# A gated mix of two attentions: the gate moved between partitions by VectorE, long transfers planned by their queue, and q, k and phi awaited by halves

## The chip, the cores and the metric

The kernel runs on one core of a Trainium2 chip. A core has TensorE (PE; its weight loads are listed as PEld), VectorE (DVE), ScalarE (ACT), GpSimd (POOL) and SyncE (SP), which here issues all DMAs, in order, on one queue. The metric is the device time of the core in microseconds, median of the runs. The profile shows one more execution, with every instruction's start and duration, and names instructions by engine and line of the kernel (L709 is line 709).

## What is computed

The reference takes x of 2048 rows by 640 and mixes the outputs of two attentions with 32 heads of 20 elements each, row by row:

```
g = sigmoid((x * gate_w).sum(-1))            # one number per row
a = A_ref(x): 4 segments of 512 rows. Per segment and head
      causal softmax attention within the segment, and
      num = phi(q) M,  den = phi(q) z + 1e-6   # memory of earlier segments
      o   = sigmoid(beta) * num/den + (1 - sigmoid(beta)) * softmax part
      M  += phi(k)^T v,  z += sum phi(k)        # phi(t) = t+1 if t>0 else exp(t)
    then @ A_wo
b = B_ref(x): causal attention in a window of 256 rows, then @ B_wo
out = g * a + (1 - g) * b
```

All inputs are float32. The softmax subtracts each row's maximum.

## The kernel before, in words

The work is cut into 16 tiles T: 4 segments s of 512 rows, and within each four groups g of 16 heads, in the order A, B, A, B (g = 0, 2, 1, 3; `head`). A tile is four units u of 4 heads, 64 units in all. For each tile PE makes the projections of q and k (`plan_qk`: five blocks m of 128 rows; L432) and of v (`plan_v`: four blocks b of 128 rows; L553), with the operands split into a high and a low part, which ACT and POOL prepare (L381, L397) from transfers that line 389 issues: x and the weights wv come by `xst`, the weights wqk and wo by `wst`, a ring of two. q and k are then split into three bfloat16 parts and stored to DRAM (`qk_store`, L487, tensors dq and dk), and read back transposed into stacks of 120 partitions (`stack_read`, L616 and L619; three reads for q and three for k per unit). In the 640 rows of q and k of a tile, rows 0 to 319 belong to its units 0 and 1, rows 320 to 639 to units 2 and 3. phi of q and k takes the same way (`phl_store`, `phi_store`; read by `mem_stack`, L756, and `mem_load`, L748).

For each unit PE computes the scores once for the maxima (`max_mm`, L644, three PSUM banks), DVE reduces them (L655), and POOL, ACT and DVE split and transpose the maxima, which go to DRAM and back as three more rows of the query stack (`max_store`, L682, tensor dmx; `max_rows`, L686). Then PE computes the scores again with the maximum subtracted (`st_mm`, L709), ACT takes the exponential (L716), POOL masks (L722), PE multiplies with v (`av_mm`, L739), DVE turns the result (L820), which is scaled, turned back and stored (o_dram, L860). The output projections load it again (L873).

The gate: `wv` of group 0 has a further column, gate_w, so that column 320 of its v projection is the gate's logit. `z_out` (L562) copies it into `zg`, rows on 128 partitions. After the fourth block, once per segment, `z_store` (L566) writes it to DRAM and `z_load` (L570) reads it back as `zc`, where partition 32h + e holds rows 32i + e, i = 0 to 15, the same for each h, as the turned outputs lie. `z_exp` (ACT, L574) and `z_sig` (DVE, L578 to L580) make g and 1 - g; `fac` and `den_mul` multiply them into the scale of the outputs.

**What sets the order.** Nothing of this is in the order of the text. Each step is handed to a planner with `add(t, engine, duration, function, ...)`, where t is when it is due in units (unit u starts at u), and `new`, `put`, `mod` and `get` name the buffers it takes, fills, changes and reads. `Plan.order` is a list scheduler: it keeps a clock for each engine and for 16 DMA rings, and issues next the step that can start first; among those that can start at the same time, the one due first. The result is one program order per engine; on the chip semaphores hold each step until its data are there. For a DMA the planner adds its cost on each ring, `size / packet / rings * (0.011 + packet / 21e3)`, to what the ring still has. The constants that matter here: AHEAD 4.26 (how many units ahead of its tile a projection is due), PACE 2.18 (how far projections may run ahead of the scores), RD 2.5 (how far ahead the stacks are read), MT 1.3 and MS 0.58 (how far ahead the maxima and their splitting are due).

Of the kernel before, what the change touches and what calls it, by code (L numbers as in the profile page):

```python
# [22 lines left out]
L = 512  # L23
# [12 lines left out]
NK, NQ, NP, NX = 4, 4, 3, 5  # L36
NMX, NPJ, NST, NW, NO = 3, 3, 2, 2, 5
NPX, NMI, NOB = 7, 2, 2
AHEAD, RD, PACE = 4.26, 2.5, 2.18
TL, OZ, WL = 1.16, 5, 0.006  # L40
P0, MA, DP, NF, NR = 3.97, 0.94, 0.0, 1, 2
MT, MS = 1.3, 0.58
WARM = 26
LM, LR, LA, AT = 0.99, 2.03, 0.0, 0.11
DM, XP, XO, XS = 0.9, 0.32, 0.2, 0.11
OA = {5: 2, 6: 3, 7: 2, 8: 2, 9: 2, 10: 2, 11: 3, 12: 3, 13: 2, 14: 2, 15: 2}
AV = ((0, 1, 2),)
EPS = 1e-6


# [4 lines left out]
class Plan:  # L55
# [38 lines left out]
    def order(self):  # L94
# [7 lines left out]
        for i, (t, _, eng, dur, fn, a, new, mod, put, get, size, pace, cols, _, bank, _, _) in enumerate(items):  # L102
            if pace == "beat":
                beats.append((t, i))
            elif pace is not None:
                j = bisect.bisect_left(beats, (t - pace, 0)) - 1
                if j >= 0:
                    deps[i].add(beats[j][1])
            def slot(name):
                k = home.get(name, name)  # L110
                s = state.setdefault(k, {"who": name, "base": None, "puts": [], "gets": []})
                assert s["who"] == name, (fn, a, name, s["who"])
                return s
            for tag, bufs, name in new:
                c = count.get(tag, 0)
                count[tag] = c + 1
                k = (tag, "slot", c % bufs)
                home[name] = k
                s = state.get(k)
                if s:  # L120
                    deps[i] |= set(s["puts"]) | set(s["gets"])
                    if s["base"] is not None:
                        deps[i].add(s["base"])
                if tag in last_new:
                    assert after[last_new[tag]] is None
                    after[last_new[tag]] = i
                    order[i] = order.get(i, 0) + 1
                last_new[tag] = i
                state[k] = {"who": name, "base": i, "puts": [], "gets": [], "free": set(deps[i])}
            if bank:  # L130
                kind[bank[2]] = bank[0]
                state[bank[2]] = {"who": bank[2], "base": i, "puts": [], "gets": [], "free": set()}
                left[bank[2]] = 1
                uses[i].append(bank[2])
            for name in (*mod, *put, *get):
                if name in left:
                    left[name] += 1
                    uses[i].append(name)
            for name in mod:
                s = slot(name)  # L140
                deps[i] |= set(s["puts"]) | set(s["gets"])
                if s["base"] is not None:
                    deps[i].add(s["base"])
                s["base"], s["puts"], s["gets"] = i, [], []
            for name in put:
                s = slot(name)
                deps[i] |= set(s["gets"])
                if s["base"] is not None:
                    deps[i] |= s["free"] if name[0] in ("q", "k", "qf", "mst", "pk") else {s["base"]}
                s["puts"].append(i)  # L150
            for name in get:
                s = slot(name)
                deps[i] |= set(s["puts"])
                if s["base"] is not None:
                    deps[i].add(s["base"])
                s["gets"].append(i)
            deps[i].discard(i)
# [22 lines left out]
        while len(out) < n:  # L180
            best = None
            for e, c in cand.items():
                cold = e == "pe" and self.cold(free[e])
                for i in c:
# [10 lines left out]
                        z = max(z, min(avail.values()))  # L195
                    if e == "dve" and "|" in items[i][2]:
                        z += DP
                    z = (z, cold and items[i][12] < 900, i)
                    if best is None or z < best[0]:
                        best = (z, e)  # L200
# [58 lines left out]


@with_exitstack
def gated_mix_kernel(ctx: ExitStack, tc: tile.TileContext, xt, wqk, wv, wo, beta, ident, out):
    nc = tc.nc
    ctx.enter_context(tc.manual_schedule())
    const = ctx.enter_context(tc.tile_pool(name="const", bufs=1))
    dram = ctx.enter_context(tc.tile_pool(name="dram", bufs=1, space=DRAM))

    o_dram = [dram.tile([H, 32, S], F32, name=f"o_dram{i}") for i in range(2)]
    attention(ctx, tc, const, dram, xt, wqk, wv, wo, beta, ident, o_dram, out)


def attention(ctx, tc, const, dram, xt, wqk, wv, wo, beta, ident, o_dram, out):
    nc = tc.nc
    wpool = ctx.enter_context(tc.tile_pool(name="weights", bufs=1))
    xpool = ctx.enter_context(tc.tile_pool(name="xs", bufs=1))
# [13 lines left out]
        for i in range(WARM):  # L289
            nc.tensor.matmul(p[:, 0:256], ones[:, 0:128], ones, start=True, stop=True)  # L290

    idf = const.tile([128, 128], F32, name="idf")

    mask_a = const.tile([128, 512], BF16, name="mask_a")
    mask_b = const.tile([128, 384], BF16, name="mask_b")

# [12 lines left out]
    gh = const.tile([128, 2, 8], F32, name="gh")  # L309

    def c_load():
        nc.sync.dma_start(idf, ident)
        nc.sync.dma_start(bet, bass.AP(tensor=beta.tensor, offset=beta.offset, ap=[[8, 4], [0, 32], [1, 8]]))

    def c_exp():
# [37 lines left out]
        nc.gpsimd.memset(kst[i][96:128, p], -1.0)  # L353

    zg = const.tile([128, 16], F32, name="zg")
    dz = [dram.tile([L], F32, name=f"dz{i}") for i in range(NSEG)]
    zc = const.tile([128, 2, 2, 16], F32, name="zc")

    plan = Plan()
# [164 lines left out]
    def plan_qk(t, dt, T, m):  # L524
# [1 line left out]
        g, s = head(T)  # L526
        plan_gemm(t, dt, k, ("x", s), wqk[g, m])
        t += NC * dt - 0.01
        ph, dk = ("phi", T, m), ("dq", T)
        plan_parts(t + 1e-4, k, k)  # L530
        add(t + 3e-4, SP, SI * len(runs_of(m)), qk_store, T, m, put=[dk], get=[("hl", k)], size=3 * 2 ** 17, packet=1024)
        nk = rows_of(m, 1) if g < 2 and s < NSEG - 1 else 0
        nq = rows_of(m, 0) if g < 2 and s else 0
        if nk or nq:
# [2 lines left out]
            add(t + 6e-5, DVE, 0.61, phi_sum, T, m, get=[k], mod=[ph])  # L537
        if nk:
            add(t + 7e-4, SP, SI * len(runs_of(m, (1,))), phi_store, T, m, get=[ph],
                new=[("dphi", 2, ("dphi", T))] if m == 1 else [], put=[("dphi", T)] if m > 1 else [], size=2048 * nk)  # L540
        if nq:
            plan_parts(t + 8e-4, ph, ph)
            add(t + 1e-3, SP, SI * len(runs_of(m, (0,))), phl_store, T, m, get=[("hl", ph)],
                new=[("dphq", 2, ("dphq", T))] if m == 0 else [], put=[("dphq", T)] if m else [], size=3072 * nq, packet=1024)

    def v_mm(T, b, c):
        if c == 0:
# [14 lines left out]
        nc.vector.tensor_copy(zg[:, 4 * s + b:4 * s + b + 1], B["v", T, b][:, 16 * DH:16 * DH + 1])  # L562


    def z_store(s):
        nc.sync.dma_start(bass.AP(tensor=dz[s].tensor, offset=dz[s].offset, ap=[[1, 4], [16, 32], [4, 4]]),  # L566
                          zg[:, 4 * s:4 * s + 4])

    def z_load(s):
        nc.sync.dma_start(zc[:, s % 2, 0], bass.AP(tensor=dz[s].tensor, offset=dz[s].offset,  # L570
                                                   ap=[[0, 4], [16, 32], [1, 16]]))

    def z_exp(s):
        nc.scalar.activation(zc[:, s % 2, 0], zc[:, s % 2, 0], AF.Exp, scale=-1.0)  # L574

    def z_sig(s):
        z = zc[:, s % 2, 0]
        nc.vector.tensor_scalar(z, z, 1.0, None, op0=ALU.add)  # L578
        nc.vector.reciprocal(z, z)
        nc.vector.tensor_scalar(zc[:, s % 2, 1], z, -1.0, 1.0, op0=ALU.mult, op1=ALU.add)  # L580

    def va(T, b):

# [3 lines left out]
    def plan_v(t, dt, T, b):  # L587
# [8 lines left out]
        if g == 0:  # L596
            add(t + 1e-4, DVE, 0.08, z_out, T, b, get=[k], put=["zg"])
            if b == 3:
                add(t + 2e-4, SP, DI, z_store, s, get=["zg"], put=[("dz", s)], size=2048, packet=4)
                add(t + 3e-4, SP, DJ, z_load, s, get=[("dz", s)], new=[("z", 2, ("z", s))], size=8192, packet=64, rings=4)  # L600
                add(t + 4e-4, ACT, 0.25, z_exp, s, mod=[("z", s)])
                add(t + 5e-4, DVE, 0.7, z_sig, s, mod=[("z", s)])

# [336 lines left out]
            add(-14 + i, POOL, 0.7, init_k, i, p, put=[("ik", i)])  # L942
    add(-13, POOL, 2.0, c_mask, put=["mk"])
    add(-25, PE, 0.107 * WARM, c_warm, bank=("warm", 1, "warm"), cols=256 * WARM)
    add(-16.5, SP, 1.1, c_load, put=["cl"], size=2 ** 16)
    add(-3, ACT, 0.25, c_exp, get=["cl"], put=["ce"])
    add(-3, DVE, 1.2, c_fac, get=["cl", "ce"], put=["cf"])

# [3 lines left out]
    for T in range(NT + 2):  # L952
# [38 lines left out]
        for u in range(4 * T, 4 * T + 4):  # L991
            tr = u - RD
            for i in range(3):
                for w in range(2):
# [1 line left out]
                    ring = [] if i else [("qk"[w] + "st", (NQ, NK)[w], k)]  # L996
                    b, c = RUNS[w][i]
                    add(tr, SP, DI, stack_read, u, w, b, c, new=ring, put=[] if ring else [k],
                        get=[("dq", T)] + ([("dq", T - NSG)] if w and back(T) else []) +
                        ([("ik", u % NK)] if ring and w else []),  # L1000
                        size=c * 8 * n, packet=2 * n if w and head(T)[0] >= 2 else 4096, rings=RINGS[c])
                    tr += 1e-3
# [8 lines left out]
    for u in range(NU):  # L1011
# [55 lines left out]
        if not isb:  # L1067
            if s > 0:
                for i in range(3):
                    qk = ("qf", u)  # L1070
                    add(u + 0.3 + 0.001 * i, SP, DI, mem_stack, u, i, get=[("dphq", T)],
                        new=[] if i else [("qf", NF, qk)], put=[qk] if i else [], size=RUNS[0][i][1] * 4096, packet=4096, rings=RINGS[RUNS[0][i][1]])
                add(te + 0.02, PE, 0.25, mem_read, u, get=[("qf", u), ("mst", T - NSG)], bank=("misc", NMI, ("num", u)),
                    cols=2048, ldw=(0.027, 0.02), lazy=LR)
                add(te + 0.03, DVE, 0.64, o_turn, u, 1, get=[("num", u)], put=[ok])
            if s < NSEG - 1:
                for i in range(4):
                    add(u - 0.3 + 0.001 * i, SP, DI, mem_load, u, i, get=[("dphi", T), "im"],
                        new=[] if i else [("pk", 1, ("pk", u))], put=[("pk", u)] if i else [], size=DH * 2048, packet=128, rings=10)
                add(u + 0.3, DVE, 0.63, mem_turn, u, get=[("pk", u)], new=[("pkn", 1, ("pkn", u))])  # L1080
                add(u + MA, PE, 0.57, mem_add, u, ldw=(0.027, 0.02), lazy=LM, get=[("pkn", u)] + [("va", T, b) for b in range(4)], bank=("madd", 1, ("madd", u)))
# [21 lines left out]
def layout(A_x, A_wq, A_wk, A_wv, A_wo, A_beta, B_x, B_wqkv, B_wo, gate_w):  # L1103
# [16 lines left out]
    def turn(w):  # L1120
        return w.reshape(NC, 128, NC, 128).transpose(2, 1, 0, 3).reshape(NC, 128, D)
    return dict(xt=n(n(A_x)[0].T), wqk=n(np.stack([turn(w) for w in qk])), wv=n(np.stack(vv)),
                wo=n(np.stack([turn(w) for w in (n(A_wo)[rows], n(B_wo)[rows], n(B_wo))])),
                beta=n(n(A_beta).reshape(8, 4).T), ident=np.eye(128, dtype=np.float32))


# [13 lines left out]
```

## Time and profile before

| what | value |
|---|---|
| median of 3 runs | 1178.53 us (1175.38 to 1179.56) |
| the profiled execution | 1183.04 us |
| its span, first to last instruction | 1181.3 us |
| granted PE clock, mean | 0.979 |
| PE, DVE, ACT, POOL busy | 93%, 66%, 60%, 69% |
| DMA moved | 224.24 MB, 190 GB/s on average |

In the views of the profile a row of a group gives line, engine, operation, tiles written <- read, shape and count, then the busy time, the mean duration of one in ns, the idle time of the engine just ahead of them and who ended it. A row of the waits gives: who waited <- for whom: us in total, times, the longest. A row of the windows gives start:end, length, then busy time (and count) of PE, PEld, DVE, ACT and POOL, the granted PE clock as a share of full speed, the busy share of the 16 DMA engines, and GB/s. A row of the instructions of a tile gives shortest/median/longest in ns, first and last start.

### The profile page before, as it was taken

What the parts mean: (1) busy time and instruction counts of PE and PEld (TensorE: products, weight loads), DVE (VectorE), ACT (ScalarE), POOL (GpSimd) and SP (SyncE); (2) the same over time, 40 slices, a digit from 0 to 9 for tenths busy, and PEclk for the clock granted to TensorE, in tenths of its full rate; (3) what the DMA queues carried; (4) which work ended last, traced back from release to release, by engine and by line L of the source; (5) the groups of instructions that cost most, each with busy time, mean ns of one, the idle gap of its engine ahead of it and who ended that gap; (6) DMA issues with size and microseconds to landing.
All of it is one profiled execution on the core that took longest, in us unless ns stands there. A gap on an engine that the chain in (4) does not pass through costs nothing.

```text
span 1181.3 us, 25003 instructions
## 1 busy us (share of the span) xinstructions
PE 1093.2 (93%) x8322; PEld 718.9 (61%) x8322; DVE 778.6 (66%) x2640; ACT 704.6 (60%) x1496; POOL 816.1 (69%) x1063
## 2 busy tenths in 40 slices
PE   9789999997999999989798999997979899999996
PEld 7565666664556666656465666665646557665564
DVE  3477887665768667976666866676647577567711
ACT  6246756675467755567454776646636477645661
POOL 9436674786568776688655877667757587756874
PEclk9989999998999999999899999999999999999999
DMA  6868878778887599777787868887588676788423
GB/s 212 171 180 195 220 195 206 186 192 183 218 204 197 143 210 253 200 193 219 160 219 188 204 167 220 209 209 178 156 171 223 172 206 160 220 202 216 137 91 107
DMA packets 194753, 224.24 MB, mean 190 GB/s; under 512 B 80768, under 2 KB 143616, under 8 KB 194624
## 3 DMA queue, kind: packets, MB, share of 16 engines
q1 hardware_dynamic: 194624, 222.64, 73.9%
q8 instruction: 66, 1.08, 0.4%
q14 instruction: 63, 0.52, 0.2%
HBM read 157.62 MB, written 64.95 MB: 188 GB/s over the span
## 4 chain that ended last, share of the span: by engine, by line
PE 52%; DMA 29%; DVE 6%; POOL 5%; ACT 3%; SPq 3%; issue 2%; POOLq 0%; DVEq 0%; ACTq 0%
PE bank L432 19%; PE bank L709 9%; PE bank L553 8%; PE bank L739 8%; PE bank L644 8%; DMA qst<-dmx 5%; DMA dmx<-mt 5%; DMA qst<-dq 4%; DMA xst<-wv 3%; DMA kst<-dk 3%; DVE bank L655 3%; DMA wst<-wqk 2%; DMA xst<-o_dram 2%; ACT P L716 1%; DMA pks<-dphi 1%
## 5 line engine op out<-in xcount | busy, mean ns | idle before, releaser
L716 ACT ACTIVATE P<-bank 128x512 f32<-128x512 f32 (+2 forms) x768 | 374.1, 559 | 121.6 <-PE bank L709 101.2
L432 PE MATMUL bank<-xhl,w 128*128 128x512 f32 x1200 | 363.8, 429 | 1.4 <-DVE xhl L397 0.4
L655 DVE CUSTOM_DVE_ANT_0 bank<-bank,mask_b 128x384 f32<-128x384 f32 (+2 forms) x512 | 260.2, 549 | 65.0 <-PE bank L644 63.9
L644 PE MATMUL bank<-kst,qst 120*128 120x384 bf16 (+3 forms) x1024 | 258.9, 314 | 33.8 <-DVE mx L655 12.8
L655 DVE CUSTOM_DVE_ANT_0 bank<-bank,mask_a 128x128 f32<-128x128 f32 (+3 forms) x512 | 238.2, 511 | 74.9 <-PE bank L644 73.6
L709 PE MATMUL bank<-qst,kst 123*128 123x384 bf16 (+2 forms) x1216 | 231.8, 293 | 38.6 <-DMA qst<-dmx 29.8
L397 POOL TENSOR_TENSOR w<-wst,w 128x640 fp32r<-128x640 f32 x119 | 185.4, 1558 | 92.5 <-ACT w L381 92.2
L432 PEld LDWEIGHTS bank<-xhl,w 128*128 128x128 f32 x1200 | 218.9, 192 | 46.1 <-issue 1.9
L722 POOL TENSOR_SCALAR_AFFINE_SELECT P<-P 128x512 f32<-128x512 f32 x256 | 161.0, 636 | 86.1 <-ACT P L716 80.2
L553 PE MATMUL bank<-wv,xhl 128*128 128x320 f32 (+1 forms) x960 | 194.9, 337 | 0.7 <-POOL wv L397 0.2
L432 PE MATMUL bank<-ohl,w 128*128 128x512 f32 x600 | 178.8, 425 | 6.5 <-POOL w L397 2.7
L709 PEld LDWEIGHTS <-kst 123*128 123x128 bf16 x1216 | 91.9, 99 | 142.3 <-issue 70.8
L644 PEld LDWEIGHTS <-qst 120*128 120x128 bf16 x1024 | 82.9, 99 | 131.1 <-issue 94.6
L739 PE MATMUL bank<-P,vau 128*32 128x384 f32 (+3 forms) x2432 | 159.9, 407 | 1.2 <-DVE mt L789 0.8
L553 PEld LDWEIGHTS bank<-wv,xhl 128*128 128x128 f32 x960 | 153.7, 192 | 11.4 <-DVE mx L655 1.4
L655 DVE DVE_READ_ACCUMULATOR2_ANT mx<- 128x1 f32 x1024 | 143.2, 140 | 0.0
L451 POOL TENSOR_TENSOR hl<-res,hl 128x512 bf16<-128x512 f32 x104 | 121.1, 1166 | 23.7 <-ACT hl L381 19.9
L820 DVE STREAM_TRANSPOSE ot<-bank 128x512 f32<-128x512 f32 x88 | 62.7, 713 | 108.5 <-PE bank L739 98.1
L432 PEld LDWEIGHTS bank<-ohl,w 128*128 128x128 f32 x600 | 109.4, 191 | 31.9 <-POOL ohl L397 4.6
L739 PEld LDWEIGHTS bank<-P,vau 128*32 128x32 f32 x2432 | 69.0, 109 | 82.3 <-issue 66.4
L381 ACT ACTIVATE w<-wst 128x640 fp32r<-128x640 f32 x121 | 89.5, 741 | 40.8 <-PE bank L432 16.3
L397 POOL TENSOR_TENSOR wv<-xst,wv 128x322 fp32r<-128x322 f32 x79 | 68.6, 878 | 48.6 <-ACT wv L381 46.7
(73 smaller groups left out, 907.9 us busy)
## 6 DMA issues: line engine op xcount, KB each, us to landing
wst<-wqk SPq DMA_DIRECT2D x80, 320.0 KB
o_dram<-ot SPq DMA_DIRECT2D x64, 256.0 KB
qst<-dq SPq DMA_DIRECT2D x64, 240.0 KB
kst<-dk SPq DMA_DIRECT2D x64, 240.0 KB
wst<-wo SPq DMA_DIRECT2D x41, 320.0 KB
xst<-wv SPq DMA_DIRECT2D x80, 161.0 KB
qst<-dq SPq DMA_DIRECT2D x64, 192.0 KB
xst<-o_dram SPq DMA_DIRECT2D x35, 256.0 KB
```

The costliest lines, as they stand in the source:

```text
L381: nc.scalar.activation(dst, src, AF.Copy)
L397: EN[e].tensor_tensor(out=t[:, 1], in0=B.pop(src), in1=f(t[:, 0]), op=ALU.subtract)
L432: nc.tensor.matmul(p, w[:, a, col:col + 128], x[:, b], start=(c == 0 and i == 0), stop=(c == NC - 1 and i == 2))
L451: EN[e].tensor_tensor(out=t[:, LO], in0=B["res", k], in1=t[:, MI], op=ALU.subtract)
L553: nc.tensor.matmul(p[:, :n], x[:, a, 128 * b:128 * b + 128], w[:, bb, :n], start=(c == 0 and i == 0), stop=(c == NC - 1 and i == 2))
L644: nc.tensor.matmul(pt[:, :n], qst[u % NQ][0:6 * DH, h, 128 * b:128 * b + 128], keys(u, 6 * DH, h, c0, n), start=True, stop=True)
L655: nc.vector.tensor_tensor_reduce(out=x, in0=x, in1=mk, scale=1.0, scalar=BIG, op0=ALU.add, op1=ALU.max, accum_out=B["M", u][:, j:j + 1])
L709: nc.tensor.matmul(pt[:, c:c + 128 * n], keys(u, 6 * DH + 3, h, c0, 128), q[0:6 * DH + 3, h, 128 * q0:128 * (q0 + n)], start=True, stop=True)
L716: nc.scalar.activation(B["P", u, b][:, 2 * p + r, c0:c1], B["st", u, b, p, r][:, c0:c1], AF.Exp, scale=SCALE)
L722: nc.gpsimd.affine_select(out=v, in_=v, pattern=[[0, 4], [1, 128]], compare_op=ALU.is_ge, fill=0.0, base=0, channel_multiplier=-1)
L739: nc.tensor.matmul(o[32 * j:32 * j + 32, 128 * q0:128 * (q0 + n)], v[:, VA * h:VA * h + 32], t[:, j, c:c + 128 * n], start=(b == 0 and i = ...
L820: nc.vector.transpose(B["ot", u][:, i].rearrange("p b e -> p (b e)"), B["o" if i == 0 else "num", u])
```

## The change

Five things change.

- The gate no longer goes through DRAM. `z_move` copies, for j = 0 to 3, the 32 partitions from 32j of `zg` to partitions 0 to 31 of `zc`; the exponential and the sigmoid work on 32 partitions in place of 128, and three copies spread the result to the other three groups of 32. All copies are on DVE.
- The planner lets a DMA whose cost on a ring is above BULK (0.3 us) start only when the fullest of its rings has no more than BACK (3 us) ahead of it.
- q and k (dq) and phi (dphi, dphq) are named by halves of the tile, so that the reads of units 0 and 1 wait, in the plan, for the blocks that hold their rows only, not for all five.
- A load of a 128 x 128 identity matrix, which nothing reads, is gone from the start.
- AHEAD, RD, PACE, MT and MS grow.

```diff
-AHEAD, RD, PACE = 4.26, 2.5, 2.18
+AHEAD, RD, PACE = 4.7, 2.9, 2.6
...
-MT, MS = 1.3, 0.58
+MT, MS = 1.5, 0.78
...
+BACK, BULK = 3, 0.3
...
                     if e == "dve" and "|" in items[i][2]:
                         z += DP
+                    if items[i][10] and items[i][10][0] > BULK:
+                        z = max(z, max(dma[:items[i][10][1]]) - BACK)
...
-    idf = const.tile([128, 128], F32, name="idf")
...
     def c_load():
-        nc.sync.dma_start(idf, ident)
...
-    dz = [dram.tile([L], F32, name=f"dz{i}") for i in range(NSEG)]
...
-        ph, dk = ("phi", T, m), ("dq", T)
+        ph = ("phi", T, m)
+
+        def halves(tag, kind):
+
+            first = lambda du: min(z for z in range(NC) for r in runs_of(z, (kind,)) if r[0] == du)
+            du = sorted({z[0] for z in runs_of(m, (kind,))})
+            return dict(new=[((tag, z), 2, (tag, T, z)) for z in du if first(z) == m],
+                        put=[(tag, T, z) for z in du if first(z) != m])
         plan_parts(t + 1e-4, k, k)
-        add(t + 3e-4, SP, SI * len(runs_of(m)), qk_store, T, m, put=[dk], get=[("hl", k)], size=3 * 2 ** 17, packet=1024)
+        add(t + 3e-4, SP, SI * len(runs_of(m)), qk_store, T, m, put=[("dq", T, z) for z in sorted({z[0] for z in runs_of(m)})], get=[("hl", k)], size=3 * 2 ** 17, packet=1024)
...
-    def z_store(s):
-        nc.sync.dma_start(bass.AP(tensor=dz[s].tensor, offset=dz[s].offset, ap=[[1, 4], [16, 32], [4, 4]]),
-                          zg[:, 4 * s:4 * s + 4])
-
-    def z_load(s):
-        nc.sync.dma_start(zc[:, s % 2, 0], bass.AP(tensor=dz[s].tensor, offset=dz[s].offset,
-                                                   ap=[[0, 4], [16, 32], [1, 16]]))
+    def z_move(s):
+        v = zc[0:32, s % 2, 0].rearrange("p (b j) -> p b j", j=4)
+        for j in range(4):
+            nc.vector.tensor_copy(v[:, :, j], zg[32 * j:32 * j + 32, 4 * s:4 * s + 4])
 
     def z_exp(s):
-        nc.scalar.activation(zc[:, s % 2, 0], zc[:, s % 2, 0], AF.Exp, scale=-1.0)
+        nc.scalar.activation(zc[0:32, s % 2, 0], zc[0:32, s % 2, 0], AF.Exp, scale=-1.0)
 
     def z_sig(s):
-        z = zc[:, s % 2, 0]
-        nc.vector.tensor_scalar(z, z, 1.0, None, op0=ALU.add)
-        nc.vector.reciprocal(z, z)
-        nc.vector.tensor_scalar(zc[:, s % 2, 1], z, -1.0, 1.0, op0=ALU.mult, op1=ALU.add)
+        z = zc[0:32, s % 2]
+        nc.vector.tensor_scalar(z[:, 0], z[:, 0], 1.0, None, op0=ALU.add)
+        nc.vector.reciprocal(z[:, 0], z[:, 0])
+        nc.vector.tensor_scalar(z[:, 1], z[:, 0], -1.0, 1.0, op0=ALU.mult, op1=ALU.add)
+        for h in range(1, 4):
+            nc.vector.tensor_copy(zc[32 * h:32 * h + 32, s % 2], z)
...
-                add(t + 2e-4, SP, DI, z_store, s, get=["zg"], put=[("dz", s)], size=2048, packet=4)
-                add(t + 3e-4, SP, DJ, z_load, s, get=[("dz", s)], new=[("z", 2, ("z", s))], size=8192, packet=64, rings=4)
+                add(t + 2e-4, DVE, 0.4, z_move, s, get=["zg"], new=[("z", 2, ("z", s))])
                 add(t + 4e-4, ACT, 0.25, z_exp, s, mod=[("z", s)])
-                add(t + 5e-4, DVE, 0.7, z_sig, s, mod=[("z", s)])
+                add(t + 5e-4, DVE, 0.9, z_sig, s, mod=[("z", s)])
...
-                        get=[("dq", T)] + ([("dq", T - NSG)] if w and back(T) else []) +
+                        get=[("dq", T, u % 4 // 2)] + ([("dq", T - NSG, u % 4 // 2)] if w and back(T) else []) +
...
-                    add(u + 0.3 + 0.001 * i, SP, DI, mem_stack, u, i, get=[("dphq", T)],
+                    add(u + 0.3 + 0.001 * i, SP, DI, mem_stack, u, i, get=[("dphq", T, g // 2)],
...
-                    add(u - 0.3 + 0.001 * i, SP, DI, mem_load, u, i, get=[("dphi", T), "im"],
+                    add(u - 0.3 + 0.001 * i, SP, DI, mem_load, u, i, get=[("dphi", T, g // 2), "im"],
```

More of the change, by code (lines that the diff above doesn't have):

```diff
@@ L152, in order @@
                 s = slot(name)
+                assert s["puts"] or s["base"] is not None, (fn, a, name)
                 deps[i] |= set(s["puts"])
@@ L261, in gated_mix_kernel @@
 @with_exitstack
-def gated_mix_kernel(ctx: ExitStack, tc: tile.TileContext, xt, wqk, wv, wo, beta, ident, out):
+def gated_mix_kernel(ctx: ExitStack, tc: tile.TileContext, xt, wqk, wv, wo, beta, out):
     nc = tc.nc
@@ L268, in gated_mix_kernel, with attention @@
     o_dram = [dram.tile([H, 32, S], F32, name=f"o_dram{i}") for i in range(2)]
-    attention(ctx, tc, const, dram, xt, wqk, wv, wo, beta, ident, o_dram, out)
-def attention(ctx, tc, const, dram, xt, wqk, wv, wo, beta, ident, o_dram, out):
+    attention(ctx, tc, const, dram, xt, wqk, wv, wo, beta, o_dram, out)
+def attention(ctx, tc, const, dram, xt, wqk, wv, wo, beta, o_dram, out):
     nc = tc.nc
@@ L539, in plan_qk @@
             add(t + 7e-4, SP, SI * len(runs_of(m, (1,))), phi_store, T, m, get=[ph],
-                new=[("dphi", 2, ("dphi", T))] if m == 1 else [], put=[("dphi", T)] if m > 1 else [], size=2048 * nk)
+                size=2048 * nk, **halves("dphi", 1))
         if nq:
@@ L543, in plan_qk @@
             add(t + 1e-3, SP, SI * len(runs_of(m, (0,))), phl_store, T, m, get=[("hl", ph)],
-                new=[("dphq", 2, ("dphq", T))] if m == 0 else [], put=[("dphq", T)] if m else [], size=3072 * nq, packet=1024)
+                size=3072 * nq, packet=1024, **halves("dphq", 0))
     def v_mm(T, b, c):
@@ L944, in attention @@
     add(-25, PE, 0.107 * WARM, c_warm, bank=("warm", 1, "warm"), cols=256 * WARM)
-    add(-16.5, SP, 1.1, c_load, put=["cl"], size=2 ** 16)
+    add(-16.5, SP, DI, c_load, put=["cl"], size=2 ** 12, packet=32)
     add(-3, ACT, 0.25, c_exp, get=["cl"], put=["ce"])
@@ L1123, in layout @@
                 wo=n(np.stack([turn(w) for w in (n(A_wo)[rows], n(B_wo)[rows], n(B_wo))])),
-                beta=n(n(A_beta).reshape(8, 4).T), ident=np.eye(128, dtype=np.float32))
+                beta=n(n(A_beta).reshape(8, 4).T))
 def kernel(**inputs):
```

## The prediction

> **What bounds the kernel now.** I read the page first, then the waits, then the chain of waits in order of time, and from there the windows around its longest links.
>
> ```profile
> span 1181.3 us, 25003 instructions
> PE 1093.2 (93%) x8322; PEld 718.9 (61%) x8322; DVE 778.6 (66%) x2640; ACT 704.6 (60%) x1496; POOL 816.1 (69%) x1063
> PE 52%; DMA 29%; DVE 6%; POOL 5%; ACT 3%; SPq 3%; issue 2%; POOLq 0%; DVEq 0%; ACTq 0%
> ```
>
> TensorE (PE) is the bound: the next engine is at 69%. The most that any reordering can win is PE's idle time, 1181.3 - 1093.2 = 88.1 us, and whatever part of its busy time ran at a reduced clock. The chain says that most of what PE waits for is transfers (29%). Who ends PE's waits:
>
> ```profile
> PE bank L709 <- DMA qst<-dmx: 29.8, 13, 7.9
> PE bank L644 <- DVE mx L655: 12.8, 12, 8.3
> PE bank L644 <- DMA kst<-dk: 6.6, 4, 1.9
> ```
>
> The largest is the row maxima (dmx) coming back from DRAM into the query stack, 29.8 us in 13 waits. That looks like an even latency problem, which planning would cure. The chain in order of time says otherwise. Of its 1907 pieces, these are the four longest transfers (start, length):
>
> ```profile
> 46.78 12.30 DMA wst<-wqk
> ...
> 271.33 11.00 DMA qst<-dmx
> ...
> 565.09 11.97 DMA xst<-wv
> ...
> 868.88 9.95 DMA dmx<-mt
> ```
>
> They are of four different kinds and sizes, so their kind isn't the cause. What they share is what SyncE (SP) had issued 0.6 to 6.2 us earlier, the store of the gate to DRAM (line 566), once per segment:
>
> ```profile
> 42.31 0.56 SPq L566 DMA_DIRECT2D dz<-zg  x1
> 265.13 0.53 SPq L566 DMA_DIRECT2D dz<-zg  x1
> 562.80 0.54 SPq L566 DMA_DIRECT2D dz<-zg  x1
> 868.30 0.52 SPq L566 DMA_DIRECT2D dz<-zg  x1
> ```
>
> The windows behind those four issues (us, busy time of the engines, granted PE clock, DMA share, GB/s):
>
> ```profile
> 44.00:56.00 12.00, 8.63 (x41) 4.52 (x40) 9.62 (x42) 0.47 (x1) 0.86 (x1) 1.00 0.83 82
> 56.00:66.20 10.20, 3.92 (x14) 3.11 (x14) 4.39 (x19) 3.69 (x8) 4.57 (x5) 0.50 0.87 252
> 268.00:277.90 9.90, 6.44 (x54) 3.51 (x52) 5.26 (x22) 1.32 (x3) 3.73 (x6) 1.00 0.88 37
> 277.90:288.10 10.20, 5.72 (x19) 3.31 (x20) 4.49 (x12) 5.30 (x12) 7.28 (x11) 0.50 0.87 255
> 566.00:574.80 8.80, 6.78 (x42) 4.76 (x42) 5.00 (x20) 4.00 (x8) 4.32 (x8) 1.00 0.60 87
> 574.80:581.60 6.80, 3.51 (x9) 2.09 (x8) 2.48 (x6) 4.43 (x12) 3.96 (x5) 0.50 0.80 190
> 870.00:882.00 12.00, 6.86 (x69) 3.88 (x67) 4.79 (x18) 2.98 (x6) 5.41 (x8) 1.00 0.73 68
> 882.00:888.80 6.80, 5.06 (x14) 2.74 (x15) 1.90 (x9) 3.00 (x9) 2.33 (x4) 0.50 0.84 216
> sum 76.70, PE 46.92 PEld 27.93 DVE 37.93 ACT 25.19 POOL 32.47; mean PE 5.86 PEld 3.49 DVE 4.74 ACT 3.15 POOL 4.06
> ```
>
> Each store is followed by 9 to 12 us in which all transfers together move 37 to 87 GB/s, while the engines stay marked busy (share 0.60 to 0.88: packets are held, not absent), and then by a catch-up at 190 to 255 GB/s. ScalarE and GpSimd starve for weights, PE runs dry, and its granted clock drops to 0.50 for the 6.8 to 10.2 us that follow. The two long dmx waits are inside these windows and have nothing to do with ordinary latency:
>
> ```profile
> 282.38 0.82 PE L709 MATMUL bank<-qst,kst 123*128 123x384 bf16 x2 [7.94 <-DMA qst<-dmx]
> ...
> 883.74 1.03 PE L709 MATMUL bank<-qst,kst 123*128 123x512 bf16 x2 [6.88 <-DMA qst<-dmx]
> ```
>
> **The change part by part.**
>
> *The gate leaves DRAM.* In the eight windows PE idles 76.70 - 46.92 = 29.8 us. All of it is waiting that the held transfers cause, so it goes with them. At clock 0.50 the 3.92 + 5.72 + 3.51 + 5.06 = 18.2 us of busy time are worth half: 9.1 us more. That the clock is real work time is seen in one matmul form, three of them at full and at half clock:
>
> ```profile
> 265.40 0.94 PE L432 MATMUL bank<-xhl,w 128*128 128x512 f32 x3
> ...
> 578.33 1.73 PE L432 MATMUL bank<-xhl,w 128*128 128x512 f32 x3
> ```
>
> Together -38.9 us. I take it whole, since the next engine's 69% leaves room to follow PE; the ends are -38.9 less what comes back (a rival, below) and a few us more for the congestion that the catch-ups leave.
>
> Is it the store, and not the weight loads beside it? The other small store of this kernel is the control:
>
> ```profile
> DMA packets 194753, 224.24 MB, mean 190 GB/s; under 512 B 80768, under 2 KB 143616, under 8 KB 194624
> dmx<-mt SPq DMA_DIRECT2D x128, 8.0 KB
> dz<-zg SPq DMA_DIRECT2D x4, 2.0 KB
> idf<-ident SPq DMA_DIRECT2D x1, 64.0 KB
> ```
>
> dmx is written 128 times in 64-byte pieces, dz 4 times in 512 pieces of 4 bytes (its access pattern ends in a step of 4 elements). Collapses of this length stand behind all four dz stores and, by the chain, behind no other kind. The Trainium skill ("DMA: Bandwidth & Descriptors", Specifications) puts the threshold for read-modify-write at 512 B. By that rule the dmx stores are as much to blame as dz, 128 against 4, and taking out dz alone would leave the trouble; the trace does not agree, since the mean rate stays at 190 GB/s around 128 such stores. What 4-byte pieces do differently I can't tell from one trace.
>
> What replaces it, per segment: four copies of 32 x 4 and three of 32 x 32 elements on VectorE (DVE). The nearest rows:
>
> ```profile
> L562 DVE COPY zg<-bank x16: 147/151/159, 26.8 to 868.1; 128x1 f32<-128x1 f32 x16
> L578 DVE TENSOR_SCALAR zc<-zc x4: 132/235/461, 65.3 to 886.0; 128x16 f32<-128x16 f32 x4
> ```
>
> Seven copies at 0.15 us, 4.2 us over four segments, or 6.6 us at 0.235; on DVE, which is at 66%. The cover is that slack; without it the maxima (L655) queued behind these copies would be late for PE by at most that sum. The exponential on ScalarE stays, and DVE still waits for it ahead of the sigmoid, with the same maxima queued behind; before, that wait ended on a transfer, now on a 0.2 us operation. I put +1 us. The Trainium skill ("VectorE: DVE Perf Modes", Two Vector instructions with no wait between them) speaks against such copies: one that starts in another group of 32 partitions than its predecessor is held until all earlier ones have ended. By that rule the copies run one by one, which is how I priced them; no run here shows it yet.
>
> SP loses eight issues of 0.5 us and the load that stood in its queue until the store had landed. The identity load (64 KB at 190 GB/s, 0.3 us) goes from the start: nothing.
>
> *Long transfers wait for short queues; halves; more lead.* These three change the planned order alone. By the planner's own cost of a DMA only dmx's and beta's remain below its 0.3 us threshold; all else is issued, by plan, when no more than 3 us are queued, so that dmx lands sooner. All six stack reads of a unit move ahead in SP's queue (past the stores of the tile's second half, and by 0.4 units, 7.4 us at 1181.3 / 64 = 18.5 us a unit), and what is queued behind a read that waits is everything else on SP, dmx included. The most that can be won: the dmx waits outside the collapses, 29.8 - 7.9 - 6.9 = 15.0 us; the key reads, 6.6; and half of the busy time in the four half-clock spells that lie elsewhere:
>
> ```profile
> 312.00:315.40 3.40, 3.02 (x8) 2.31 (x8) 2.26 (x11) 0.71 (x2) 0.47 (x2) 0.50 0.68 124
> ...
> 929.80:933.20 3.40, 3.40 (x14) 1.57 (x12) 1.14 (x4) 2.54 (x6) 0.00 (x0) 0.50 0.68 195
> sum 13.70, PE 13.05 PEld 7.75 DVE 7.75 ACT 8.67 POOL 5.30; mean PE 3.26 PEld 1.94 DVE 1.94 ACT 2.17 POOL 1.33
> ```
>
> that is 6.5; in all -28 us. A loss has no bound in the rows, since a later load can starve any engine; I take the rival's +21.6 for it. Between these ends I take -5, a third of the dmx waits: what remains of them is 11 waits of 1.4 us on average, spread over the whole run, and the reads that now stand further ahead in SP's queue work against the shorter transfer queue. What is late next is the bank of a maximum that DVE has not yet read (L644, below).
>
> **The sum.** The profiled execution took 1183.04 us (span 1181.3 and 1.7 around it). 1183.0 - 38.9 + 1 - 5 = 1140.1. It is 4.5 us above the median of the runs, so against 1178.53 the same -42.9 gives 1135.6, say 1136.
>
> **The rivals.**
>
> *Planning pays in full* (0.17). The collapses go and so do the 28 us: 1178.5 - 38.9 + 1 - 28 = 1112.6. For it: the dmx waits are the largest group. Against it: the rest of PE's idle time is in pieces with many releasers.
>
> *A new wait takes half back* (0.15). Maxima are planned 0.2 units earlier and projections 0.44, with the same eight PSUM banks and three for maxima. L644's waits for DVE without the 8.3 of the first collapse are 4.5 us in 11, 0.41 each. Were every one of the 64 units to have one, that is 26.2, or 21.7 more than now: 1136 + 21.7 = 1157.7.
>
> *It isn't the store* (0.05). The collapse belongs to the weight loads that are in flight at the end of a gate tile, and stays. By the 512 B rule of the Trainium skill's page above the time comes out here too. Then only the copies and planning count: 1178.5 + 1 - 5 = 1174.5. Against it: those loads come for each of the 16 tiles, the collapses 4 times.
>
> *Long transfers come too late, slower* (0.04). PE eats weights from a ring of two:
>
> ```profile
> L381 ACT ACTIVATE w<-wst 128x640 fp32r<-128x640 f32 x121 | 89.5, 741 | 40.8 <-PE bank L432 16.3
> L432 PE MATMUL bank<-xhl,w 128*128 128x512 f32 x1200 | 363.8, 429 | 1.4 <-DVE xhl L397 0.4
> ```
>
> Each of the 121 loads is a long transfer that the new rule may hold back. Once they are late by more than their slack, PE waits 121 times. From (42.9 + 5.9) / 121 = 0.40 us each it decides the sign; at 0.8 us the time is 1136 + 97 = 1233. Against it: PE idles just 1.4 us ahead of 1200 such matmuls, so loads now come well ahead, and the 3 us left queued keep the transfers going.
>
> **How the numbers follow.** The forecast itself has 0.59, with 1122 to 1150 for the planning's share between -19 and +9. The range must reach into the rivals on both sides: down to full planning, 1112 less 2 for the spread of the runs, up to the new wait, 1158. Outside lie 0.05 + 0.04 and the tails of the others. A difference of 0.5% (5.9 us) is about what a measurement of this kernel can tell from none. Faster by more: 0.59 + 0.17 + 0.15 = 0.91; within: 0.05; slower: 0.04.
>
> **What would show it.** Right: no stretch of 8 us below 90 GB/s between 30 and 1090 us; no half-clock spell of 6.8 us or more in the middle; no chain link of 9 us; PE's idle time near 50 us, its clock at 0.99 or over; the dmx waits at 10 us; seven small DVE copies of about 0.15 us per segment. Wrong: collapses that stay (the store wasn't it); the collapses gone but waits of L644 for DVE or of L432 for weights grown by tens of us.

## The result, and the profile after

The changed kernel takes 1128.85 us (median of 4 runs, 1123.76 to 1134.08) against 1176.95 us for the kernel before beside it (1168.55 to 1179.56): a ratio of 0.9603, 95% interval 0.9535 to 0.9672, 46.7 us by the ratio. The forecast was 1136. Its profiled execution took 1123.76 us, with a granted clock of 0.997 (0.979 before).

The page of the changed kernel:

```profile
span 1122.0 us, 24995 instructions
PE 1076.4 (96%) x8322; PEld 714.1 (64%) x8322; DVE 788.2 (70%) x2667; ACT 707.4 (63%) x1500; POOL 813.5 (73%) x1060
DMA packets 192017, 224.13 MB, mean 200 GB/s; under 512 B 78160, under 2 KB 140880, under 8 KB 191888
```

PE's idle time is 1122.0 - 1076.4 = 45.6 us, from 88.1, and its busy time is 16.8 us less for the same matmuls: that is mostly the clock (before, PE was busy for 31 us at half clock, now for 7, so 12 us of the 16.8). Who ends PE's waits now:

```profile
PE bank L714 <- DMA qst<-dmx: 17.9, 17, 2.4
PE bank L649 <- ACT P L721: 6.4, 7, 2.6
PE bank L714 <- DVE ot L825: 3.5, 2, 2.1
```

L714 is the line that was L709, L649 the one that was L644. The longest wait was 8.3 us and is 2.6. The waits of L644 for DVE (12.8 us) and for key reads (6.6) are gone but for 0.4 us. The maxima from DRAM still lead, in more and shorter waits than before.

The gate's new steps, and four windows of 12 us around the places where they run (columns as explained with the profile before):

```profile
L575 DVE COPY zc<-zg x16: 119/574/1110, 36.9 to 828.5; 32x4 f32<-32x4 f32 x16
L586 DVE COPY zc<-zc x12: 170/174/812, 40.5 to 831.7; 32x32 f32<-32x32 f32 x12
```

```profile
40.00:52.00 12.00, 10.95 (x89) 6.89 (x88) 11.85 (x53) 4.94 (x11) 4.20 (x6) 1.00 0.96 274
252.00:264.00 12.00, 10.18 (x108) 6.39 (x101) 9.38 (x30) 8.77 (x23) 9.38 (x14) 1.00 0.86 232
530.00:542.00 12.00, 12.00 (x106) 8.28 (x103) 10.34 (x36) 8.37 (x23) 8.87 (x15) 1.00 0.55 157
820.00:832.00 12.00, 12.00 (x106) 8.63 (x96) 9.23 (x33) 6.21 (x15) 9.08 (x15) 1.00 0.84 208
```

Where 37 to 87 GB/s moved before, it is now 157 to 274, at full clock.

### The profile page after: what moved, and what is told of

It reads as the page before. It is cut to its first block, busy times and chain, and to the rows that moved or that the text cites. A ratio compares the mean times of both kernels' runs of the same rounds, so it can differ in the third digit from the quotient of the medians.

```text
span 1122.0 us, 24995 instructions
## 1 busy us (share of the span) xinstructions
PE 1076.4 (96%) x8322; PEld 714.1 (64%) x8322; DVE 788.2 (70%) x2667; ACT 707.4 (63%) x1500; POOL 813.5 (73%) x1060
## 5 line engine op out<-in xcount | busy, mean ns | idle before, releaser
L660 DVE CUSTOM_DVE_ANT_0 bank<-bank,mask_b 128x384 f32<-128x384 f32 (+2 forms) x512 | 259.4, 554 | 42.9 <-PE bank L649 41.7
L649 PE MATMUL bank<-kst,qst 120*128 120x384 bf16 (+3 forms) x1024 | 257.4, 312 | 7.7 <-ACT P L721 6.4
L714 PE MATMUL bank<-qst,kst 123*128 123x384 bf16 (+2 forms) x1216 | 227.5, 288 | 23.1 <-DMA qst<-dmx 17.9
L714 PEld LDWEIGHTS <-kst 123*128 123x128 bf16 x1216 | 89.9, 98 | 126.1 <-issue 68.8
L560 PEld LDWEIGHTS bank<-wv,xhl 128*128 128x128 f32 x960 | 152.8, 190 | 13.7 <-POOL wv L397 2.4
L660 DVE DVE_READ_ACCUMULATOR2_ANT mx<- 128x1 f32 x1024 | 145.7, 142 | 0.0
L649 PEld LDWEIGHTS <-qst 120*128 120x128 bf16 x1024 | 82.3, 98 | 97.3 <-issue 64.1
L381 ACT ACTIVATE hl<-res 128x512 bf16<-128x512 f32 x104 | 66.0, 635 | 25.7 <-DVE res L444 13.5
```

What stands on the lines that cost most here:

```text
L381: nc.scalar.activation(dst, src, AF.Copy)
L560: nc.tensor.matmul(p[:, :n], x[:, a, 128 * b:128 * b + 128], w[:, bb, :n], start=(c == 0 and i == 0), stop=(c == NC - 1 and i == 2))
L649: nc.tensor.matmul(pt[:, :n], qst[u % NQ][0:6 * DH, h, 128 * b:128 * b + 128], keys(u, 6 * DH, h, c0, n), start=True, stop=True)
L660: nc.vector.tensor_tensor_reduce(out=x, in0=x, in1=mk, scale=1.0, scalar=BIG, op0=ALU.add, op1=ALU.max, accum_out=B["M", u][:, j:j + 1])
L714: nc.tensor.matmul(pt[:, c:c + 128 * n], keys(u, 6 * DH + 3, h, c0, 128), q[0:6 * DH + 3, h, 128 * q0:128 * (q0 + n)], start=True, stop=True)
```

## The experiments

Two theories. Theory 1 is the prediction's: the gate's store holds up all transfers, and that is most of the gain. Theory 2: the new order and lead carry most of it. The runs, each against the kernel before on the same chip (the interval is that of the ratio; PE's idle time and the clock are those of the one profiled execution, which can be the fastest of a kernel's runs, as for the changed kernel and gate only, or the slowest, as for halves undone and the rule on all):

| kernel | median us | ratio to before | PE idle us | clock |
|---|---|---|---|---|
| before | 1176.95 | 1 | 88.1 | 0.979 |
| changed | 1128.85 | 0.9603 (0.9535 to 0.9672) | 45.6 | 0.997 |
| gate only | 1152.93 | 0.9796 (0.9765 to 0.9826) | 62.2 | 0.994 |
| changed, gate undone | 1160.01 | 0.9845 (0.9809 to 0.9880) | 72.2 | 0.977 |
| changed, no rule for long transfers | 1152.82 | 0.9788 (0.9757 to 0.9818) | 55.6 | 0.988 |
| changed, lead as before | 1136.46 | 0.9646 (0.9616 to 0.9676) | 48.8 | 0.998 |
| changed, halves undone | 1132.47 | 0.9617 (0.9574 to 0.9660) | 49.3 | 0.991 |
| changed + dead store, 4-byte pieces, dense | 1161.35 | 0.9863 (0.9813 to 0.9913) | 68.1 | 0.977 |
| changed + dead store, 4-byte pieces, 512 bytes apart | 1137.80 | 0.9650 (0.9594 to 0.9705) | 54.3 | 0.987 |
| changed + dead store, 16-byte pieces | 1133.25 | 0.9639 (0.9592 to 0.9686) | 49.7 | 0.992 |
| gate and rule only | 1142.52 | 0.9706 (0.9672 to 0.9739) | 53.6 | 0.994 |
| changed, BACK 1 | 1530.97 | 1.3012 (1.2958 to 1.3065) | 266.1 | 0.906 |
| changed, BACK 8 | 1143.79 | 0.9719 (0.9683 to 0.9755) | 52.9 | 0.992 |
| changed, rule on all transfers | 1140.16 | 0.9700 (0.9663 to 0.9737) | 57.7 | 0.986 |

**The gate alone, and all but the gate.** The first takes z_move and the new z_exp and z_sig into the kernel before; the second puts z_store and z_load back into the changed one.

```diff
...
+                add(t + 2e-4, DVE, 0.4, z_move, s, get=["zg"], new=[("z", 2, ("z", s))])
-                add(t + 2e-4, SP, DI, z_store, s, get=["zg"], put=[("dz", s)], size=2048, packet=4)
-                add(t + 3e-4, SP, DJ, z_load, s, get=[("dz", s)], new=[("z", 2, ("z", s))], size=8192, packet=64, rings=4)
...
```

> The kernel before with one part of the change: the gate by VectorE copies, no dz store and no dz load; all else, the lead constants and the identity load too, as before. Theory 1 (the store of 4-byte pieces holds the transfers, and that is most of the gain): the four collapses are gone, PE idle falls from 88 to about 58 us, the half-clock spells of 6.8 us and more are gone, time 1177 - 38 = 1139 us, between 1132 and 1147. Theory 2 (the new order and lead are most of the gain, the collapse would be paid elsewhere anyway): 1160 us or more.

> The changed kernel with the gate through DRAM again, all else as changed. Theory 1: four stretches of 8 us and more below 90 GB/s behind the four stores, and 1129 + 38 = 1167 us, or some less if the longer lead of the new order covers a part of each stretch. Theory 2: 1140 us or less.

The first falls between the two theories, the second near theory 1. The gate alone is worth 1 - 0.9796, 24 us; all the rest alone 1 - 0.9845, 18 us; each on top of the other 28.5 and 22.7. So the gate carries 51 to 61% of the 46.7 us: the larger part, but not the 38 us of theory 1. The collapses do go with the gate (with the gate alone, 12 us from 40, 258, 552 and 843 us, behind the moves, have 203 to 261 GB/s) and come back with it. The first of the four with the gate undone, with the 13.7 us behind it, and the third:

```profile
45.00:53.00 8.00, 8.00 (x47) 5.53 (x45) 8.00 (x37) 2.72 (x5) 3.11 (x4) 1.00 0.86 66
53.00:56.50 3.50, 1.44 (x7) 0.69 (x5) 2.26 (x8) 0.94 (x2) 0.86 (x1) 1.00 0.69 174
56.50:66.70 10.20, 4.04 (x15) 3.26 (x16) 1.87 (x10) 2.47 (x7) 3.85 (x5) 0.50 0.89 238
...
554.30:562.30 8.00, 4.65 (x60) 2.52 (x59) 2.46 (x9) 0.86 (x2) 1.50 (x2) 0.96 0.77 42
```

That PE is busy for all of the first 8.00 us doesn't mean that the longer lead covers the collapse: PE runs dry just behind them (1.44 of 3.50, then 4.04 of 10.20 at half clock, where the kernel before had 3.92 of 10.20). And in the kernel with the gate alone, PE's waits show what takes a part back:

```profile
PE bank L706 <- DMA qst<-dmx: 13.1, 10, 3.2
PE bank L641 <- DVE mx L652: 11.3, 17, 2.0
```

L641 is the L644 of before: its waits for DVE are 11.3 us in 17, where outside the first collapse they were 4.5 in 11.

**The rule and the lead.**

```diff
-BACK, BULK = 3, 0.3
+BACK, BULK = 3, 1e9
```

> The changed kernel without the rule for long transfers (BULK so high that no transfer counts as long). Theory 1 with its planning share of -5: 1129 to 1134 us, the dmx waits of PE 18 to 23 us. Theory 2 (the rule carries the rest of the gain by landing dmx sooner): 1140 us or more, with dmx waits above 25 us.

> The changed kernel with the five lead constants of before (AHEAD 4.26, RD 2.5, PACE 2.18, MT 1.3, MS 0.58). Theory 1: 1129 to 1134 us. Theory 2 (the lead carries the rest of the gain): 1140 us or more, with PE waiting for key reads (kst<-dk, 6.6 us before) and for maxima again.

> The changed kernel with every read of q, k and phi planned behind all five blocks of its tile, as before; all else as changed. If the halves carry a part of the planning's gain: 1135 us or more, with PE waiting for key reads or dmx at the first two units of the tiles. If the rule for long transfers carries it all: 1126 to 1132 us.

Undoing the rule costs 0.9788 - 0.9603, 21.8 us, so theory 2 holds for it. The dmx waits rose to 22.1 us only, in the band of theory 1; the cost is elsewhere too: PE idle +10.0 us, and a clock of 0.988 in place of 0.997, which over 1145 us is 10 us more. Undoing the lead or the halves costs 5.1 and 1.6 us by the ratios, with intervals that overlap that of the changed kernel: neither is told from nothing, and both times lie between the bands that the two answers would have given.

**The store by itself.** Three kernels add to the changed one a store of `zg` per segment that nothing reads.

```diff
...
+        nc.sync.dma_start(bass.AP(tensor=dz[s].tensor, offset=dz[s].offset, ap=[[1, 4], [16, 32], [4, 4]]),
+                          zg[:, 4 * s:4 * s + 4])
...
# 512 bytes apart (dz 128 times as long): ap=[[128, 4], [2048, 32], [512, 4]];  16-byte pieces: ap=[[4, 128], [1, 4]]
```

> The changed kernel with a store added that nothing reads: once per segment the gate's logits go to DRAM in 512 pieces of 4 bytes, into 2 KB, by the access pattern of the old store. Theory 1 (the store alone, not its load, holds the transfers): four stretches of 6 us and more below 90 GB/s behind the four stores, 1129 + 24 to 31 = 1153 to 1160 us. Rival (the load that follows, or SP waiting for the store to land, is the trouble): no such stretch, 1129 to 1132 us.

> As the kernel with the dead store, but each 4-byte piece goes 512 bytes from the next, so that no two share a 64-byte line. If the small size of the pieces is the trouble (each a read-modify-write, by the rule of the Trainium skill's page on DMA): stretches and time as with the dense store, 1153 to 1160 us. If it is that many pieces fall into the same lines: no stretches, 1129 to 1133 us.

> As the kernel with the dead store, but the same 2 KB go out in 128 pieces of 16 bytes, side by side. If the number of pieces and of writes into one line decides (four to a 64-byte line in place of sixteen): stretches a quarter as long, 2 to 3 us, and 1129 to 1140 us. If any piece below 64 bytes does it: stretches as with the dense store.

Windows of 8 us, from 2.6 us behind each store, first for the dense pieces, then for those 512 bytes apart:

```profile
45.00:53.00 8.00, 7.50 (x43) 4.92 (x42) 8.00 (x34) 2.03 (x5) 1.38 (x2) 1.00 0.73 55
265.50:273.50 8.00, 7.06 (x88) 3.84 (x86) 7.42 (x29) 2.86 (x6) 5.83 (x6) 1.00 0.77 99
552.00:560.00 8.00, 5.08 (x62) 2.64 (x61) 4.44 (x14) 1.38 (x5) 1.54 (x2) 0.94 0.78 35
860.30:868.30 8.00, 6.06 (x30) 3.84 (x30) 5.33 (x23) 5.98 (x15) 6.54 (x8) 1.00 0.89 114
```

```profile
46.00:54.00 8.00, 7.78 (x44) 5.23 (x42) 8.00 (x34) 4.18 (x8) 5.58 (x7) 1.00 0.69 185
260.50:268.50 8.00, 7.92 (x94) 4.48 (x93) 7.39 (x32) 3.94 (x9) 6.75 (x9) 1.00 0.84 223
543.00:551.00 8.00, 8.00 (x80) 4.75 (x81) 7.33 (x24) 5.92 (x15) 5.66 (x9) 1.00 0.54 140
840.50:848.50 8.00, 6.23 (x33) 4.00 (x32) 7.01 (x25) 5.19 (x13) 5.00 (x6) 1.00 0.66 177
```

A dense store costs 0.9863 - 0.9603, 30.6 us in four issues, with no load behind it; two of its four collapses are as deep as before, two milder (99 and 114 GB/s). The lowest 6 us behind each store have 25 to 79 GB/s, so all four are there; the time is 1.4 us above the band of theory 1. The same 512 pieces of 4 bytes at 512 bytes cost 5.5 us by the ratios (0.9650; the time is 4.7 us above the band without stretches), 128 pieces of 16 bytes side by side 4.2 (0.9639), both with intervals that overlap the changed kernel's. So it is neither the size of the pieces nor their number alone, but many small pieces close together: the dense store puts sixteen, from four groups of partitions, into each 64 bytes, and against the store 512 bytes apart the place of the pieces is all that differs. The 16-byte store changes their size, number and order at once. Whether the 64 bytes, the whole 2 KB or the order of the pieces is what counts isn't separated. The Trainium skill's threshold for read-modify-write ("DMA: Bandwidth & Descriptors", Specifications: below 512 B) would blame all three alike; these runs do not agree.

The packet records of the traces show that other transfers are held, and not only that SP can't issue. Behind the old stores single packets of the two weight transfers (1288 bytes for wv, 2560 for wqk), which over the whole run last 56 and 102 ns at the median, last up to 8.0 us; behind the spread store up to 1.2.

**What the rule for long transfers does.**

> The kernel before with two parts of the change: the gate by VectorE and the rule for long transfers. Halves, lead and the identity load as before. If these two carry the gain and the rest only adds what the single undoings showed (3.6 for the halves, 7.6 for the lead): 1133 to 1142 us. If the rule needs the halves or the lead to work at all: near the gate alone, 1148 us or more.

> The changed kernel with BACK 1 in place of 3: long transfers are planned only when at most 1 us is queued. Theory (the rule works because SP is not stuck behind earlier long transfers when the maxima are ready): 1124 to 1134 us, the maxima's store at most as late as with 3. Rival (the rule starves the transfers when it is made tight): 1140 us or more, with a lower mean GB/s and PE waiting for weights or reads.

> The changed kernel with BACK 8 in place of 3. Theory: most of the rule's effect is lost, 1140 to 1152 us, and more units than the 8 of the changed kernel have their turned maxima wait over 1 us for the store (27 without the rule). Rival (3 us or 8 us is the same, the rule only reshuffles): 1126 to 1134 us.

> The changed kernel with the rule on all transfers, the maxima's too (BULK 0). If the gain comes from SP's queue being short for everyone: 1126 to 1134 us, as with the rule on long ones alone. If it comes from the maxima passing the long transfers in SP's order: 1138 us or more, with the maxima's store late in more units.

The rule works without halves and lead: gate and rule alone give 34.6 of the 46.7 us; lead, halves and the missing identity load together the other 12, with intervals that just touch. But the parts aren't independent. On top of the gate the rule alone is worth 0.9796 - 0.9706, 10.6 us, and lead and halves without the rule 0.9796 - 0.9788, nothing; on top of gate, lead and halves the rule is worth 21.8. About half of its worth comes only with them. BACK 8 loses 0.0116 (13.7 us), so how short the queue must be matters. The rule on all transfers loses 0.0097 (11.4 us); the intervals overlap by 0.0009, but all six times are above the slowest of the changed kernel, so it is likely, not certain, that the maxima have to pass the others. BACK 1 costs 402 us against the changed kernel.

SP's queue shows what the rule changes. In the trace SP's DMAs carry eight semaphores strictly in turn, so the ninth DMA can't be issued before the first has landed. Here is SP without the rule, while unit 0's maxima, transposed by 56.34 us, wait to be stored (L687):

```profile
52.64 0.43 SPq L624 DMA_DIRECT2D qst<-dq  x1
53.12 0.33 SPq L624 DMA_DIRECT2D kst<-dk  x1
...
55.73 0.27 SPq L624 DMA_DIRECT2D kst<-dk  x1
56.95 0.27 SPq L624 DMA_DIRECT2D qst<-dq  x1
57.97 0.32 SPq L624 DMA_DIRECT2D kst<-dk  x1
58.50 0.31 SPq L624 DMA_DIRECT2D qst<-dq  x1
59.45 0.27 SPq L624 DMA_DIRECT2D kst<-dk  x1
60.34 0.36 SPq L389 DMA_DIRECT2D wst<-wqk  x1
60.88 0.36 SPq L389 DMA_DIRECT2D xst<-wv  x1
62.03 0.33 SPq L389 DMA_DIRECT2D wst<-wqk  x1
63.21 0.57 SPq L687 DMA_DIRECT2D dmx<-mt  x1
```

The first reads are issued some 0.4 us apart; from 55.73 on it is 0.5 to 1.2 us, each when the transfer eight before it has landed, and the 8 KB store stands 6.9 us behind them. In the changed kernel unit 0's maxima are transposed by 52.49 us, and the store is issued 0.03 us later, ahead of the next reads:

```profile
52.52 0.57 SPq L687 DMA_DIRECT2D dmx<-mt  x1
53.15 0.48 SPq L624 DMA_DIRECT2D qst<-dq  x1
53.67 0.32 SPq L624 DMA_DIRECT2D kst<-dk  x1
```

Over the whole run, from the end of each unit's transposition (L681) to the issue of its first store: more than 1 us in 27 of 64 units without the rule (78.9 us in all), in 26 with BACK 8 (72.3), in 20 with the rule on all (46.1), in 8 in the changed kernel (16.7), in none with BACK 1; in the kernel before, 23 (66.4), with the gate alone 21 (59.8), with gate and rule 11 (22.5). Among kernels that differ in the rule alone, time and lateness go together, down to BACK 1. That the late store is what costs the time isn't shown, though: PE's waits for the maxima don't follow it. With BACK 8 they are shorter than the 17.9 us of the changed kernel, and the way from SP's order to PE's time stays open:

```profile
PE bank L714 <- DMA qst<-dmx: 16.1, 13, 3.1
```

With BACK 1 the prediction's slower rival is at work:

```profile
DMA packets 192017, 224.13 MB, mean 147 GB/s; under 512 B 78160, under 2 KB 140880, under 8 KB 191888
```

```profile
SPq L687 <- DVE mt L681: 386.6, 55, 15.4
```

```profile
PE bank L714 <- DMA qst<-dmx: 43.6, 15, 7.8
PE bank L432 <- ACT w L381: 35.1, 16, 5.5
PE bank L432 <- POOL w L397: 34.4, 34, 3.9
```

With 1 us the plan holds each long transfer until nearly nothing is on its way, and puts it behind the store of the maxima in SP's order; SP then stands 386.6 us waiting for DVE's transpose with reads and weights behind it, the same bytes take longer (147 GB/s in place of 200), and PE waits for weights. The setting of 3 us lies between two walls. A setting between 3 and 8 wasn't tried, and no kernel here beat the changed one.

## Why the prediction was right, and where its steps were off

- **Range, sign and cause of the largest part: right.** The four collapses are behind the dz stores, go with them, and a store alone brings them back. The rival that it isn't the store falls. What the prediction left open, why 4-byte pieces do it, is answered in part: they lie close together.
- **The gate's term, -38.9, was too large: 24 us alone, 28.5 on top of the rest.** Three things failed. The sum was made on one execution at the upper end of its spread (1183.04 us; the median here is 1176.95): profile against profile, the kernel with the gate alone has 25.9 us less idle time and a span 34.3 us shorter (1181.3 to 1147.0), near the forecast, but its profiled 1148.76 us is also the lowest of its six runs. "All of it is waiting that the held transfers cause" was too much: in the changed kernel PE still idles 48.00 - 45.13 = 2.9 us in the four windows of 12 us, so by estimate 4.6 of the 29.8 us weren't the store's. And "I take it whole" was wrong: PE, freed, runs into DVE's maxima (+6.8 us), which is the rival "a new wait takes half back" in small; it goes only with the new order.
- **The copies, +1: too short in the rows, not measured by themselves.** They run one by one, as priced, but all 28 take 11.7 us in place of 4.2 to 6.6 (last section). In the changed kernel PE's waits for DVE's maxima are 1.5 us in all, so DVE's slack covers them there.
- **The planning's term, -5: mis-sized, 18 us alone and 22.7 on top of the gate.** The step that failed is "a third of the dmx waits". I looked for the gain in one group of PE's waits. That group did not shrink (15.0 us outside the collapses, now 17.9); from the kernel with the gate alone to the changed one the gain is spread over waits for DVE (L644's, 11.3 us to 0.4), key reads (3.6 to none) and the clock (0.994 to 0.997), and about half of it comes with the rule alone. I read SP's queue only as a latency of transfers; how much of the gain its order is stays open. A sign of it stood in the waits of SP's queue in the kernel before. A read of q or k does not need another read's data, yet line 619 waits for its landing:

```profile
SPq L619 <- DMA kst<-dk: 18.4, 26, 1.8
SPq L619 <- DMA qst<-dq: 15.6, 22, 2.3
```

  In the changed kernel these waits are 5.8 and 3.0 us, but without the rule 6.7 and 4.6, so they don't price the rule.

- **The two errors have opposite signs** (10 to 15 us too much, 13 to 18 too little). The total of -42.9 against -46.7 by the ratio owes its closeness to that.
- **The signs named.** No half-clock spell of 6.8 us is left, idle time is 45.6 (said: near 50), the clock 0.997: as forecast. Dmx waits of 10 us and copies of 0.15 us: not. "No stretch of 8 us below 90 GB/s" isn't met to the letter: from 166.6 us the rate is 88, from 1079 us 79. But there the DMA engines are busy for 0.37 and 0.23 only and PE for 8.00 of 8.00, so little is asked for and PE doesn't wait; the sign should have named the DMA share too. The chain of waits couldn't be read: in the changed kernel it could be followed back over a small part of the span only.
- **The slower rival** had the right mechanism, but at a setting that the change doesn't have: it was priced at 97 us, and BACK 1 costs 402.

## What to carry to other kernels

Look at the bytes moved per microsecond around the longest links of the chain, not only at who waits: a 2 KB store of 512 scattered 4-byte pieces, invisible in every ranking, cost this kernel 24 to 31 us in four issues. Where a queue holds a fixed number of transfers in flight, as this one's eight, look at the order of issue as well as at sizes: here a store of 8 KB stood 6.9 us behind a batch of long transfers, and the rule that keeps such batches short was worth 10.6 to 21.8 us, while making them wait too long for it cost 402. And a sum made on one execution carries that execution's luck; compare its time with the median before taking its stalls whole.

## What the runs showed of the hardware that wasn't expected

Small copies on DVE wait for GpSimd. Four copies of 32 x 4 elements in the changed kernel, and POOL at the same time:

```profile
535.41 1.58 DVE L575 COPY zc<-zg 32x4 f32<-32x4 f32 x4
```

```profile
534.98 0.64 POOL L727 TENSOR_SCALAR_AFFINE_SELECT P<-P 128x512 f32<-128x512 f32 x1
535.56 0.64 POOL L730 TENSOR_SCALAR_AFFINE_SELECT P<-P 128x512 f32<-128x512 f32 x1
536.16 0.22 POOL L670 TENSOR_TENSOR mx<-mx 128x16 f32<-128x16 f32 x1
536.33 0.64 POOL L727 TENSOR_SCALAR_AFFINE_SELECT P<-P 128x512 f32<-128x512 f32 x1
```

The four copies end at 535.63, 536.22, 536.40 and 536.99 us, each some 20 ns behind the end of a POOL instruction that began before it. Where POOL is idle such a copy takes 0.16 us (the one at 39.42 us), beside POOL up to 1.11. The Trainium skill says this of a port pair that VectorE's two-port copies share with GpSimd ("SBUF — State Buffer", Who interferes with whom: whoever starts first has it for the whole instruction), and the trace agrees. It does not matter here; a chain of such copies on the critical path would pay one POOL instruction each.
